# A small product on quarters of the matmul array, with its result sent through DRAM: one change to a gated pair of linear attentions

## The chip, the cores and the metric

The kernel runs on one core of a Trainium2 chip. The metric is the device time of one execution in microseconds (us). All runs told of here were in the fast state, at a granted TensorE clock of 1.0 unless the text says otherwise (the granted clock is the share of its full clock that the chip lets TensorE run at). A ratio is the mean time of one kernel's fast runs over the mean of the fast runs of the kernel before in the same rounds, with a 95% interval; it is therefore not quite the ratio of the medians that are quoted beside it.

## The reference, cut to what matters

Two branches, A and B, of linear attention read the same x (2048 rows of 640) with weights of their own. A gate mixes their outputs.

```python
def _A_ref(x, wqkv, wo):                 # _B_ref is the same with B's weights
    B, S, D = x.shape                    # 1, 2048, 640
    H = 32; Dh = D // H                  # 32 heads of 20
    q, k, v = ...                        # x @ wqkv, split in heads
    phi = lambda t: jnp.where(t > 0, t + 1, jnp.exp(t)) + 1e-6
    pq, pk = phi(q), phi(k)
    kv = jnp.einsum("bhsd,bhse->bhde", pk, v)
    z = jnp.einsum("bhsd->bhd", pk)
    num = jnp.einsum("bhqd,bhde->bhqe", pq, kv)
    den = jnp.einsum("bhqd,bhd->bhq", pq, z)[..., None] + 1e-6
    return ... (num / den) ... @ wo

g = _sigmoid((x * gate_w).sum(-1, keepdims=True))
return g * a + (1 - g) * b
```

The kernel uses that everything behind pq is linear. It first forms G = pk^T x (640 by 640). KV is the part of G and wv within each head, 32 blocks of 20 by 20. Then W' = KV wo (640 by 640) is made once a branch, so that each row tile of the output is one product of the scaled pq with W'.

## The kernel before

A small list scheduler in the file orders the operations. Its order on TensorE is the order of the program text. The parts that the change and the argument touch:

```python
GR = 120      # rows of a unit: six heads
NU = 6        # five units of 120 rows, and a sixth of which 40 are used
...
    # KV: for each unit, wv's columns against G; VectorE masks what is not in a head's block
    def kv_unit(X):
        ...
        for us in ((0, 1, 2, 3), (4, 5)):
            ...
                for i, u in enumerate(us):
                    lo = GR * u if u < 5 else D - GR
                    for c in range(NC):
                        r = e.matmul(
                            PS[0:GR, ps.slot, GR * i : GR * i + GR],
                            WV[X][:, c, lo : lo + GR],
                            gv[:, c, :, lo // 5 : lo // 5 + 24],
                            start=(c == 0),
                            stop=(c == NC - 1),
                        )
...
    # W': one product a unit on the whole array, copied by ScalarE, then copied to its layout
    def wp_unit(X, u):
        ...
            e.matmul(a[0:GR, 0:512], KVL[X][:, u, :], WO[X][:, u, 0:512], start=True, stop=True)
            return e.matmul(a[0:GR, 512:D], KVL[X][:, u, :], WO[X][:, u, 512:D], start=True, stop=True)
        ...
            lambda e: e.activation(WST[X][:, u, :], psw(ps, D)[0:GR, :], ACT.Copy),
        ...
        dma("SP", ..., WP[X][lo // 5 : hi // 5, :, :], WST[X][r:GR, u, :], ...)
...
    # the output: A's part of the first NOA row tiles is kept in SBUF in fp32; B's part is added later
    NOA = 13
    ...
    for u in range(NU):
        wp_unit("B", u)
        if u % 2 == 0:
            o_part(5 + u // 2)
    for t in range(8, NOA):
        o_part(t)
    ...
    for t in range(NOA):
        o_rest(t)                        # B's part, and VectorE's add
    ...
    for t in range(NOA, NT - 1):
        out_unit(t)                      # A and B in one accumulation, ScalarE's copy
    out_last(NT - 1)
```

## Time and profile before

| | before |
|---|---|
| median of the first 3 runs | 188.89 us (188.58 to 189.0) |
| span of the profiled run | 187.6 us |
| TensorE busy | 184.6 us, 98% |
| VectorE, ScalarE busy | 72%, 51% |

TensorE never waits after the first 5.1 us. The first tile of B in the output stage reads the W' of B that was made last. In the lines of profiles below, PE is TensorE, PEld its weight loads, DVE VectorE, ACT ScalarE, POOL GpSimd and SP SyncE; a q behind a name means the engine's instruction queue, and L904 is line 904 of the kernel. The timeline of TensorE in the kernel before shows no gap there (start, duration in us, engine, line, operation, output and inputs, count):

```profile
158.15 1.52 PE L904 MATMUL ps<-WPA,PKA 128*128 128x512 bf16 x10
159.51 0.71 PE L904 MATMUL ps<-WPB,PKA 128*128 128x512 bf16 x4
```

Ten matmuls of one tile are spaced over 1.36 us (their durations overlap, so the group shows 1.52), and 158.15 + 1.36 is 159.51: the first matmul on WPB follows at once.

### The profile page before, as it was taken

To read this page: it belongs to the slowest core of one execution; us is meant where nothing else is said; L and a number is where in the kernel's file an instruction comes from. 1 tells how busy PE (TensorE), PEld (TensorE's weight loads), DVE (VectorE), ACT (ScalarE), POOL (GpSimd) and SP (SyncE) were. 2 spreads that over 40 slices of the span, in tenths; PEclk is the share of its full clock that TensorE was granted. 3 is DMA by queue.
4 is the path that set the end of the run, shared out by engine and by line. 5 is a ranking of instruction groups with operands and counts; after the bars stand their busy time and mean duration, and the time that the engine had idled before them with its cause. 6 is when DMAs were issued, how large, how long until landed. Compare 5 with 4: busy or idle time off the path is not lost.

```text
span 187.6 us, 3202 instructions
## 1 busy us (share of the span) xinstructions
PE 184.6 (98%) x1261; PEld 107.9 (58%) x1261; DVE 135.4 (72%) x260; ACT 95.6 (51%) x171; POOL 0.8 (0%) x8
## 2 busy tenths in 40 slices
PE   8999999999999999999999999999999999999995
PEld 4555555555555656665557556655556655555552
DVE  2388888888833555487798999879996999965600
ACT  5365655556554546544675667877524594100012
POOL 1000000000000000000000000000000000000000
PEclk9999999999999999999999999999999999999999
DMA  7999999996001011011701222540015165132322
GB/s 185 293 163 158 252 392 364 344 214 136 4 0 35 0 38 35 0 35 24 92 10 31 56 49 48 124 116 3 0 35 118 32 153 134 39 140 105 136 79 70
DMA packets 36301, 19.89 MB, mean 106 GB/s; under 512 B 25630, under 2 KB 36286, under 8 KB 36286
## 3 DMA queue, kind: packets, MB, share of 16 engines
q1 hardware_dynamic: 35844, 19.48, 41.6%
q8 instruction: 10, 0.16, 0.4%
q10 hardware_dynamic: 442, 0.20, 0.4%
q14 instruction: 5, 0.04, 0.1%
HBM read 9.39 MB, written 2.62 MB: 64 GB/s over the span
## 4 chain that ended last, share of the span: by engine, by line
PE 96%; DMA 2%; SPq 0%; DVE 0%; issue 0%; DVEq 0%
PE ps L904 23%; PE ps L744 23%; PE ps L513 18%; PE ps L618 18%; PE ps L619 5%; PE ps L514 5%; DMA WKW<-in_A_wqkv_dram 2%; PE ps L660 2%; PE ps L698 1%; SPq L343 0%; PE ps L699 0%; DVE TSB L948 0%; DVEq L230 0%; PE ps L494 0%
## 5 line engine op out<-in xcount | busy, mean ns | idle before, releaser
L513 PE MATMUL ps<-WKW,XT 128*128 128x512 bf16 x160 | 44.4, 381 | 0.3 <-DMA WKW<-in_A_wqkv_dram 0.3
L761 ACT ACTIVATE EK<-ps 128x512 bf16<-128x512 f32 x40 | 23.9, 598 | 31.5 <-PE ps L744 29.4
L514 PE MATMUL ps<-WKW,XT 128*128 128x128 bf16 (+1 forms) x160 | 35.2, 220 | 0.0
L546 ACT ACTIVATE EK<-ps 128x640 bf16<-128x640 f32 x32 | 22.4, 704 | 10.8 <-DVE EK L549 5.9
L513 PEld LDWEIGHTS ps<-WKW,XT 128*128 128x128 bf16 x160 | 15.7, 98 | 19.8 <-DMA WKW<-in_A_wqkv_dram 0.6
L744 PE MATMUL ps<-XT,WQA 128*128 128x512 bf16 x100 | 24.5, 379 | 0.0
L744 PE MATMUL ps<-XT,WQB 128*128 128x512 bf16 x100 | 23.7, 379 | 0.0
L618 PE MATMUL ps<-XN,PKB 128*128 128x512 bf16 x80 | 23.5, 379 | 0.0
L618 PE MATMUL ps<-XN,PKA 128*128 128x512 bf16 x80 | 23.5, 379 | 0.0
L771 DVE TENSOR_SCALAR EK<-EK 128x512 bf16<-128x512 bf16 x40 | 11.6, 291 | 14.9 <-ACT EK L761 14.8
L619 PE MATMUL ps<-XN,PKA 128*128 128x129 bf16 x80 | 17.6, 220 | 0.0
L619 PE MATMUL ps<-XN,PKB 128*128 128x129 bf16 x80 | 17.6, 220 | 0.0
L904 PE MATMUL ps<-WPA,EX 128*128 128x512 bf16 x120 | 17.3, 299 | 0.0
L904 PE MATMUL ps<-WPB,PKA 128*128 128x512 bf16 x120 | 16.5, 299 | 0.0
L744 PEld LDWEIGHTS ps<-XT,WQB 128*128 128x128 bf16 x100 | 10.9, 117 | 8.5
L514 PEld LDWEIGHTS ps<-WKW,XT 128*128 128x128 bf16 x160 | 15.8, 98 | 0.0
L549 DVE TENSOR_SCALAR EK<-EK 128x640 bf16<-128x640 bf16 x32 | 10.4, 326 | 7.1 <-ACT EK L546 7.1
L744 PEld LDWEIGHTS ps<-XT,WQA 128*128 128x128 bf16 x100 | 10.6, 117 | 8.1
L618 PEld LDWEIGHTS ps<-XN,PKA 128*128 128x128 bf16 x80 | 9.4, 118 | 7.9
L618 PEld LDWEIGHTS ps<-XN,PKB 128*128 128x128 bf16 x80 | 9.4, 117 | 7.8
L950 ACT ACTIVATE TSB<-ps 128x640 bf16<-128x640 f32 (+1 forms) x3 | 2.0, 668 | 23.2 <-PE ps L904 23.2
L557 DVE SCALAR_TENSOR_TENSOR PKA<-ps,EK 128x640 bf16<-128x640 f32 x16 | 13.2, 825 | 0.6
(77 smaller groups left out, 239.9 us busy)
## 6 DMA issues: line engine op xcount, KB each, us to landing
out_dram<-TSB SPq DMA_DIRECT2D x15, 160.0 KB, 1.8
XN<-in_A_x_dram SPq DMA_DIRECT2D x1, 2240.0 KB, 9.0
WKW<-in_A_wqkv_dram SPq DMA_DIRECT2D x5, 160.0 KB, 4.2
WKW<-in_B_wqkv_dram SPq DMA_DIRECT2D x5, 160.0 KB, 4.0
WQA<-in_A_wqkv_dram SPq DMA_DIRECT2D x1, 800.0 KB, 10.7
WQB<-in_B_wqkv_dram SPq DMA_DIRECT2D x1, 800.0 KB, 11.9
WVA<-in_A_wqkv_dram SPq DMA_DIRECT2D x1, 800.0 KB, 12.7
WVB<-in_B_wqkv_dram SPq DMA_DIRECT2D x1, 800.0 KB, 14.3
```

Of the source, the lines that this page charges most:

```text
L513: e.matmul(a[:, 0:512], l, WK[X][:, c, 0:512], start=(c == 0), stop=(c == NC - 1))
L514: return e.matmul(a[:, 512:w], l, WK[X][:, c, 512:w], start=(c == 0), stop=(c == NC - 1))
L546: op("ACT", lambda e: e.activation(EK[:, ek.slot, :], psw(ps, D), ACT.Exp), act_cost(D), ins=[ps] + first, outs=[ek], name="ke")
L549: lambda e: e.tensor_scalar(EK[:, ek.slot, :], EK[:, ek.slot, :], 1.0, EPS, op0=ALU.min, op1=ALU.add),
L557: lambda e: e.scalar_tensor_tensor(PKt[X][:, t, :], psw(ps, D), 0.0, EK[:, ek.slot, :], op0=ALU.max, op1=ALU.add),
L618: e.matmul(a[:, 0:512], l, XN[:, t, 0:512], start=(t == 0), stop=(t == NT - 1))
L619: return e.matmul(a[:, 512 : D + 1], l, XN[:, t, 512 : D + 1], start=(t == 0), stop=(t == NT - 1))
L660: r = e.matmul(PS[0:GR, ps.slot, GR * i : GR * i + GR], WV[X][:, c, lo : lo + GR], gv[:, c, :, lo // 5 : lo // 5 + 24], start=(c == 0), st ...
L744: r = e.matmul(PS[:, ps.slot, :], WQ[X][:, c, g::5], XT[:, c, 512 * b : 512 * b + 512], start=(c == 0), stop=(c == NC - 1),)
L761: lambda e: e.activation(EQ[:, eq.slot, :], PS[:, ps.slot, :], ACT.Exp),
L771: lambda e: e.tensor_scalar(EQ[:, eq.slot, :], EQ[:, eq.slot, :], 1.0, EPS, op0=ALU.min, op1=ALU.add),
L904: r = e.matmul(a[:, l0 - lo : h0 - lo], PQ[X, b][:, g, 128 * (t % 4) : 128 * (t % 4) + 128], WP[X][:, g, l0:h0], start=(X == first and g = ...
```

## The change

The intent is to use the array better in W'. A unit of W' has at most 120 rows in six blocks of 20 by 20, so most of the 128 by 128 array multiplies zeros. The change takes 60 by 60 blocks and puts four of them on the four 64 by 64 quarters of the array. All of W' of a branch is then done in two bursts of 320 output columns each. W' goes from its staging tile to its layout through DRAM, in five stores and one load, in place of six copies inside SBUF. KV gets full 128-column weights and a narrow last unit. Fifteen row tiles of A are kept instead of 13. Four padding rows that the 64-row layout needs are loaded.

```diff
-                    lo = GR * u if u < 5 else D - GR
                     for c in range(NC):
+                        lo, n, w = (GR * u, 128, 24) if u < 5 else (540, 104, 8)
                         r = e.matmul(
-                            PS[0:GR, ps.slot, GR * i : GR * i + GR],
-                            WV[X][:, c, lo : lo + GR],
-                            gv[:, c, :, lo // 5 : lo // 5 + 24],
+                            PS[0:n, ps.slot, GR * i : GR * i + NC * w],
+                            WV[X][:, c, lo : lo + n],
+                            gv[:, c, :, 24 * u : 24 * u + w],
...
+    def wp_burst(X, half):
+        ps = [Buf("wp", "ps", 2) for _ in range(2)]
+        lo = HALF * half
+        def fn(e):
+            for k in range(3):
+                for a, b in ((0, 192), (192, HALF)) if k == 1 else ((0, HALF),):
+                    for t in range(4 * k, min(4 * k + 4, 11)):
+                        c, r, u = t // 2 % 2, t % 2 if t < 10 else 1, t // 2
+                        w, p = (64 - 4 * r, HR) if t < 10 else (40, 40)
+                        d = HR * r if t < 10 else 0
+                        o = PS[64 * c : 64 * c + p, ps[r].slot : ps[r].slot + 2, :].rearrange("p a b -> p (a b)")
+                        x = e.matmul(
+                            o[:, HALF * k + a : HALF * k + b],
+                            KVL[X][64 * r : 64 * r + w, u, d : d + p],
+                            WO[X][64 * r : 64 * r + w, u, lo + a : lo + b],
...
+            for c in range(2):
+                st(X, r, c, 3 * r, 2 if c else 3, HR, 120 * c + HR * r)
+            if r:
+                st(X, r, 2, 5, 1, 40, 600)
+        if half == 1:
+            last_ld[0] = dma("SP", "wpl" + X, WP[X][:, :, :], WPD[X].rearrange("(p g) n -> p g n", g=NC), 819200, ...)
...
-    NOA = 13
+    NOA = 15
...
-    for u in range(NU):
-        wp_unit("B", u)
-        if u % 2 == 0:
-            o_part(5 + u // 2)
+    wp_burst("B", 0)
+    o_part(5)
+    o_part(6)
+    wp_burst("B", 1)
+    o_part(7)
     for t in range(8, NOA):
         o_part(t)
+    ft_op[2].behind, ft_op[3].behind = last_st[0], last_ld[0]
```

Cut are the masks, the loads of wo by halves of 60 rows, the scheduler's constants and the pads, and some reordering: KV of B one tile earlier, W' of A at other places of its loop, one copy raised in priority, two scalings of B held behind adds. The last line orders two of B's four factor transposes (the DMA transposes of the scaling factors of its row blocks) on SyncE's queue: the third behind the last store, the fourth behind the load.

More of the change, by code (lines that the diff above doesn't have):

```diff
@@ L20 @@
 NU = 6
+HR = 60
+HALF = 320
 def _bf16_bits(a):
@@ L30, in _consts @@
     p = np.arange(128)[:, None]
-    bd = (p // 20 == np.arange(24)[None, :] // 4).astype(np.float32)
-    return _bf16_bits(bd)
-CW = 24
+    q, m = p % 64, np.arange(24)[None, :]
+    bd = np.where(p < 64, (q >= 4) & ((q - 4) // 20 == m // 4), (q < 60) & (3 + q // 20 == m // 4))
+    be = q // 20 == m[:, 0:8] // 4
+    return _bf16_bits(np.concatenate([bd, be], axis=1).astype(np.float32))
+CW = 32
 XS_W = 672
@@ L40, with __init__ @@
 class Buf:
-    def __init__(self, name, pool=None, n=1):
-        self.name, self.pool, self.n = name, pool, n
+    def __init__(self, name, pool=None, n=1, at=(0, 2, 4, 6)):
+        self.name, self.pool, self.n, self.at = name, pool, n, at
         self.writers, self.readers = [], []
@@ L107, in can @@
                 w = max(w, d.end + (HOP if d.eng != o.eng or d.dma else 0.0))
+            skip = set()
             for b in o.outs:
                 if b.pool and b.slot is None:
-                    got = self.pick(b, w)
+                    got = self.pick(b, w, skip)
                     if got is None:
@@ L113, in can @@
                     w = max(w, got[0])
+                    skip |= set(range(got[1], got[1] + b.n))
             return w
@@ L144, in run @@
                 at[e] = w + o.dma[0]
-                o.end = max(w + o.dma[0] + 1500.0, bus[0]) + o.dma[1] / o.dma[2]
+                o.end = max(w + o.dma[0] + o.dma[3], bus[0]) + o.dma[1] / o.dma[2]
                 bus[0] = o.end
@@ L163, in run, with pick @@
         return max(o.end for o in self.ops)
-    def pick(self, b, t):
+    def pick(self, b, t, skip=()):
         pool = self.free[b.pool]
@@ L169, in pick @@
         for x in pool:
-            have[x[1]] = x[0]
+            if x[1] not in skip:
+                have[x[1]] = x[0]
         if b.n == 1:
-            if not pool:
+            if not have:
                 return None
@@ L176, in pick @@
             return best[0], best[3]
-        c = [(max(have[s], have[s + 1]), s) for s in have if s % 2 == 0 and s + 1 in have]
+        c = [(max(have[i] for i in range(s, s + b.n)), s) for s in b.at if all(i in have for i in range(s, s + b.n))]
         return min(c) if c else None
@@ L275, in body @@
     WQ = {X: sb("WQ" + X, [128, NC, D], bf) for X in XS}
-    WV = {X: sb("WV" + X, [128, NC, D], bf) for X in XS}
-    WO = {X: sb("WO" + X, [GR, NU, D], bf) for X in XS}
+    WV = {X: sb("WV" + X, [128, NC, D + 8], bf) for X in XS}
+    WO = {X: sb("WO" + X, [128, NU, D], bf) for X in XS}
     PK = {X: sb("PK" + X, [128, NT * D], bf) for X in XS}
@@ L296, in body @@
     GS = {X: sb("GS" + X, [128, NC, D], bf) for X in XS}
-    KVL = {X: sb("KVL" + X, [GR, NU, GR], bf) for X in XS}
-    WST = {X: WKW[0:GR, i * NU * D : (i + 1) * NU * D].rearrange("p (u f) -> p u f", u=NU) for i, X in enumerate(XS)}
+    KVL = {X: sb("KVL" + X, [128, NU, GR], bf) for X in XS}
+    WST = {X: WKW[:, i * NU * D : (i + 1) * NU * D].rearrange("p (u f) -> p u f", u=NU) for i, X in enumerate(XS)}
     WP = {X: sb("WP" + X, [128, NC, D], bf) for X in XS}
@@ L303, in body @@
     FXT = {"A": WV["A"][:, :, :].rearrange("p c f -> p (c f)")[:, 0:2048].rearrange("p (b s) -> p b s", b=NB), "B": XNf[:, 0:2048].rearrange("p (b s) -> p b s", b=NB)}
-    NOA = 13
+    NOA = 15
     OA = [XNf[:, 2048 + 1280 * i : 3328 + 1280 * i].bitcast(f32) for i in range(6)]
-    OA += [PK["B"][:, 1280 * i : 1280 * i + 1280].bitcast(f32) for i in range(7)]
+    OA += [PK["B"][:, 1280 * i : 1280 * i + 1280].bitcast(f32) for i in range(8)]
+    OA += [XT[:, :, :].rearrange("p c s -> p (c s)")[:, 0:1280].bitcast(f32)]
     NEK, NEQ, NOS = 4, 4, 4
@@ L328, in body @@
     IDN = sb("IDN", [128, 128], bf)
-    BDM = CST[0:GR, 0:24]
+    BDM = CST[:, 0:24]
+    BDE = CST[64:104, 24:32]
     sch = Sched({"ps": 8, "ek": NEK, "eq": NEQ, "os": NOS})
@@ L339, in dma @@
     def dma(q, name, dst, src, nbytes, ins=(), outs=(), after=(), issue=450.0, transpose=False, prio=None):
+        timing = (330.0, 1500.0) if not transpose else (140.0, 1500.0) if loading else (1000.0, 1150.0)
         def fn(e):
@@ L343, in fn @@
                 return e.dma_start(d, src() if callable(src) else src, transpose=transpose)
-        o = op(q, fn, 0.0, ins, outs, after, prio=prio, name=name, dma=(issue, nbytes, 95.0 if transpose else 330.0))
+        o = op(q, fn, 0.0, ins, outs, after, prio=prio, name=name, dma=(issue, nbytes) + timing)
         if loading:
@@ L369, in body @@
     bwv = {X: Buf("wv" + X) for X in XS}
-    bwo = {X: Buf("wo" + X) for X in XS}
+    bwo = {}
     op("DVE", lambda e: e.memset(ONE[:, :], 1.0), 120.0, outs=[bone], name="one")
@@ L386, in body @@
     zgw = op("POOL", lambda e: e.memset(GWZ[:, :], 0.0), 200.0, name="zgw")
+    bpad = {X: Buf("pad") for X in XS}
+    for X in XS:
+        op("POOL", lambda e, X=X: e.memset(WV[X][:, :, 0:4], 0.0), 300.0, outs=[bpad[X]], prio=10**6, name="wvpad")
     bxo = Buf("xo")
@@ L403, in xt_dma @@
             outs=bxt[t0:t1],
-            issue=(t1 - t0) * 850.0,
+            issue=(t1 - t0) * 1250.0,
             transpose=True,
@@ L427, in body @@
     for X in XS:
-        dma("SP", "wv" + X, WV[X][:, :, :], w3(X, 2), 819200, outs=[bwv[X]])
+        dma("SP", "wv" + X, WV[X][:, :, 4 : D + 4], w3(X, 2), 819200, outs=[bwv[X]])
     for X in XS:
-        bo5 = Buf("wo5" + X)
-        dma("SP", "wo" + X, WO[X][:, 0:5, :], wo[X][0:600, :].rearrange("(u p) n -> p u n", p=GR), 768000, outs=[bwo[X]])
-        dma("SP", "wo5" + X, WO[X][:, 5, :], wo[X][520:640, :], 153600, outs=[bo5])
-        bwo[X, 5] = bo5
+        for r in range(2):
+            bwo[X, r] = Buf("wo")
+            dma(
+                "SP",
+                "wo%s%d" % (X, r),
+                WO[X][4 + HR * r : 64 + HR * r, 0:5, :],
+                wo[X][0:600, :].rearrange("(u r p) n -> r p u n", r=2, p=HR)[r],
+                384000,
+                outs=[bwo[X, r]],
+            )
+        bwo[X, 2] = Buf("wo")
+        dma("SP", "wopad" + X, WO[X][0:4, 0:5, :], wo[X][0:4, :].unsqueeze(1).to_broadcast([4, 5, D]), 25600, outs=[bpad[X]])
+        dma("SP", "wo2" + X, WO[X][64:104, 5, :], wo[X][600:640, :], 51200, outs=[bwo[X, 2]])
     loading.clear()
@@ L633, in g_unit @@
             outs=[z],
+            prio=-1,
             name="zc",
@@ L643, in g_unit @@
             outs=[bgs[X, g]],
-            issue=850.0,
+            issue=1250.0,
             transpose=True,
@@ L652, in kv_unit, with out @@
         gv = GS[X][:, :, :].rearrange("p c (g m) -> p c g m", g=NC)
-        for us in ((0, 1, 2, 3), (4, 5)):
-            ps = Buf("kv", "ps")
-            def fn(e, us=us, ps=ps):
-                for i, u in enumerate(us):
-                    lo = GR * u if u < 5 else D - GR
-                    for c in range(NC):
-                        r = e.matmul(
-                            PS[0:GR, ps.slot, GR * i : GR * i + GR],
-                            WV[X][:, c, lo : lo + GR],
-                            gv[:, c, :, lo // 5 : lo // 5 + 24],
-                            start=(c == 0),
-                            stop=(c == NC - 1),
-                        )
-                return r
-            o = op("PE", fn, 5 * len(us) * mm_cost(GR), ins=[bwv[X]] + [bgs[X, g] for g in range(NC)], outs=[ps], name="kv" + X)
-            if X == "A":
-                kv_op[X].append(o)
+        def out(src, u0, n, w, mask, r0, r1):
             b = Buf("kvl")
             bkvl[X].append(b)
-            n = len(us)
             op(
                 "DVE",
-                lambda e, us=us, ps=ps, n=n: e.tensor_tensor(
-                    out=KVL[X][:, us[0] : us[0] + n, :].rearrange("p u (m g) -> p u g m", g=NC),
-                    in0=PS[0:GR, ps.slot, 0 : GR * n].rearrange("p (u g m) -> p u g m", u=n, g=NC),
-                    in1=BDM.unsqueeze(1).unsqueeze(1).to_broadcast([GR, n, NC, 24]),
+                lambda e: e.tensor_tensor(
+                    out=KVL[X][r0:r1, u0 : u0 + n, 0 : w * NC].rearrange("p u (m g) -> p u g m", g=NC),
+                    in0=src().rearrange("p (u g m) -> p u g m", u=n, g=NC),
+                    in1=mask.unsqueeze(1).unsqueeze(1).to_broadcast([r1 - r0, n, NC, w]),
                     op=ALU.mult,
                 ),
-                dve1(GR * n),
+                dve1(w * NC * n),
                 ins=[ps, bcst],
@@ L688, in kv_unit @@
             )
-    bwp = {}
-    bwpm = {X: [] for X in XS}
-    def wp_unit(X, u):
-        ps = Buf("wp", "ps", 2)
-        def fn(e):
-            a = psw(ps, D)
-            e.matmul(a[0:GR, 0:512], KVL[X][:, u, :], WO[X][:, u, 0:512], start=True, stop=True)
-            return e.matmul(a[0:GR, 512:D], KVL[X][:, u, :], WO[X][:, u, 512:D], start=True, stop=True)
-        op(
-            "PE",
-            fn,
-            mm_cost(512) + mm_cost(128),
-            ins=[bkvl[X][u // 4], bwo[X] if u < 5 else bwo[X, 5]],
-            outs=[ps],
-            name="wp%s%d" % (X, u),
-        )
-        b = Buf("wst")
-        op(
-            "ACT",
-            lambda e: e.activation(WST[X][:, u, :], psw(ps, D)[0:GR, :], ACT.Copy),
-            act_cost(D),
-            ins=[ps],
-            outs=[b],
-            prio=-1,
-            name="wpc",
-        )
-        bwp[X, u] = b
-        d = Buf("wpm")
-        bwpm[X].append(d)
-        r = 80 if u == 5 else 0
-        lo, hi = GR * u, min(D, GR * u + GR)
-        dma(
-            "SP",
-            "wpm%s%d" % (X, u),
-            WP[X][lo // 5 : hi // 5, :, :],
-            WST[X][r:GR, u, :],
-            1280 * (hi - lo),
-            ins=[b],
-            outs=[d],
-            issue=850.0,
@@ new lines, in kv_unit, with fn @@
+        for us in ((0, 1, 2, 3), (4, 5)):
+            ps = Buf("kv", "ps")
+            def fn(e, us=us, ps=ps):
+                for i, u in enumerate(us):
+                    for c in range(NC):
+                        lo, n, w = (GR * u, 128, 24) if u < 5 else (540, 104, 8)
+                        r = e.matmul(
+                            PS[0:n, ps.slot, GR * i : GR * i + NC * w],
+                            WV[X][:, c, lo : lo + n],
+                            gv[:, c, :, 24 * u : 24 * u + w],
+                            start=(c == 0),
+                            stop=(c == NC - 1),
+                        )
+                return r
+            o = op("PE", fn, 5 * len(us) * 55.0, ins=[bwv[X], bpad[X]] + [bgs[X, g] for g in range(NC)], outs=[ps], name="kv" + X)
+            if X == "A":
+                kv_op[X].append(o)
+            n = min(us[-1], 4) - us[0] + 1
+            out(lambda ps=ps, n=n: PS[:, ps.slot, 0 : GR * n], us[0], n, 24, BDM, 0, 128)
+            if 5 in us:
+                out(lambda ps=ps: PS[64:104, ps.slot, GR : GR + 40], 5, 1, 8, BDE, 64, 104)
@@ new lines, in body @@
+    bwst = {(X, r): Buf("wst") for X in XS for r in range(2)}
+    bwps = {X: [] for X in XS}
+    WPD = {X: nc.dram_tensor("wps" + X, [D, D], bf, kind="Internal").ap() for X in XS}
+    bwpm = {X: [Buf("wpm")] for X in XS}
+    def wp_burst(X, half):
+        ps = [Buf("wp", "ps", 2) for _ in range(2)]
+        lo = HALF * half
+        def fn(e):
+            for k in range(3):
[9 more added lines that the diff above has]
+                            WO[X][64 * r : 64 * r + w, u, lo + a : lo + b],
+                            start=True,
+                            stop=True,
+                        )
+            return x
+        op("PE", fn, 640.0, ins=bkvl[X] + [bwo[X, i] for i in range(3)] + [bpad[X]], outs=ps, name="wp%s%d" % (X, half))
+        for r in range(2):
+            dst = WST[X][0:124, 3 * r : 3 * r + 3, lo : lo + HALF]
+            src = lambda r=r: psw(ps[r], 3 * HALF)[0:124, :].rearrange("p (k n) -> p k n", k=3)
+            op(
+                "ACT",
+                lambda e, dst=dst, src=src: e.activation(dst, src(), ACT.Copy),
+                act_cost(3 * HALF),
+                ins=[ps[r]],
+                outs=[bwst[X, r]],
+                prio=-1 if X == "A" else None,
+                name="wpc",
+            )
+            if half == 0:
+                continue
+            for c in range(2):
[3 more added lines that the diff above has]
+        if half == 1:
+            last_ld[0] = dma("SP", "wpl" + X, WP[X][:, :, :], WPD[X].rearrange("(p g) n -> p g n", g=NC), 819200, ins=bwps[X], outs=bwpm[X], prio=-1)
@@ new lines, in body, with st @@
+    last_st, last_ld = [None], [None]
+    def st(X, r, c, slot, n, rows, row):
+        h = 64 * min(c, 1)
+        b = Buf("wps")
+        bwps[X].append(b)
+        last_st[0] = dma(
+            "SP",
+            "wps%s%d%d" % (X, r, c),
+            bass.AP(tensor=WPD[X].tensor, offset=WPD[X].offset + D * row, ap=[[D, rows], [240 * D, n], [1, D]]),
+            WST[X][h : h + rows, slot : slot + n, :],
+            1280 * rows * n,
+            ins=[bwst[X, r]],
+            outs=[b],
+            issue=450.0,
@@ L833, in den @@
                 after=[red_op[b]] if b in red_op else (),
-                issue=900.0,
+                issue=1250.0,
                 transpose=True,
@@ L874, in den @@
                 after=kv_op[X],
-                issue=900.0,
+                issue=1250.0,
                 transpose=True,
@@ L920, in o_mm @@
         )
-    boa = {}
+    boa, adds = {}, {}
     def o_part(t):
@@ L938, in o_post @@
         if eng == "ADD":
-            op(
+            adds[t] = op(
                 "DVE",
@@ L1004, in f @@
             elif g == 2:
+                if k == 1:
+                    wp_burst("A", 0)
                 q_next(1)
-                wp_unit("A", 2 * k)
-                wp_unit("A", 2 * k + 1)
             elif g == 3:
+                if k == 0:
+                    wp_burst("A", 1)
                 q_next(2)
@@ L1022, in body @@
     den("B")
+    kv_unit("B")
     o_part(3)
-    kv_unit("B")
     o_part(4)
-    for u in range(NU):
-        wp_unit("B", u)
-        if u % 2 == 0:
-            o_part(5 + u // 2)
+    wp_burst("B", 0)
[3 more added lines that the diff above has]
+    o_part(7)
     for t in range(8, NOA):
         o_part(t)
+    ft_op[2].behind, ft_op[3].behind = last_st[0], last_ld[0]
     for b in range(3):
@@ L1041, in body @@
     out_last(NT - 1)
+    for h in range(2):
+        pqs_op["B", 3, h].behind = adds[3 + h]
     span = sch.run()
```

## The prediction

> **What bounds the kernel now.** I read the page's busy shares first, then the slices, then the chain that ended last, then the waits of TensorE, then the groups and the timeline around the two places that the change touches. The busy shares, the first two rows of slices and the chain:
>
> ```profile
> PE 184.6 (98%) x1261; PEld 107.9 (58%) x1261; DVE 135.4 (72%) x260; ACT 95.6 (51%) x171; POOL 0.8 (0%) x8
> ...
> PE   8999999999999999999999999999999999999995
> ...
> PE 96%; DMA 2%; SPq 0%; DVE 0%; issue 0%; DVEq 0%
> PE ps L904 23%; PE ps L744 23%; PE ps L513 18%; PE ps L618 18%; PE ps L619 5%; PE ps L514 5%; DMA WKW<-in_A_wqkv_dram 2%; PE ps L660 2%; PE ps L698 1%; SPq L343 0%; PE ps L699 0%; DVE TSB L948 0%; DVEq L230 0%; PE ps L494 0%
> ```
>
> TensorE is on the chain for 96% of 187.6 us. The page cautions that a busy PE is not PE at its peak, so the waits of TensorE come next. They are all there are:
>
> ```profile
> PE ps L444 <- DVE ONE L372: 0.4, 1, 0.4
> PE ps L513 <- DMA WKW<-in_A_wqkv_dram: 0.3, 1, 0.3
> ```
>
> Both lie in the first 5.1 us. From there to the last matmul the kernel is one stream of matmuls, and a change pays only by shortening the stream or costs by opening a hole in it. The groups that the change touches are W' (lines 698 and 699) and KV (line 660); the timeline shows what they cost as spacing, which is what counts, since durations overlap:
>
> ```profile
> L698 PE MATMUL ps<-WOB,KVLB 120*120 120x512 bf16 x6 | 2.1, 380 | 0.0
> L699 PE MATMUL ps<-WOB,KVLB 120*120 120x128 bf16 x6 | 1.3, 217 | 0.0
> L660 PE MATMUL ps<-GSB,WVB 128*120 128x120 bf16 x30 | 1.8, 218 | 0.0
> ...
> 115.22 0.38 PE L698 MATMUL ps<-WOA,KVLA 120*120 120x512 bf16 x1
> 115.44 0.22 PE L699 MATMUL ps<-WOA,KVLA 120*120 120x128 bf16 x1
> 115.49 0.38 PE L698 MATMUL ps<-WOA,KVLA 120*120 120x512 bf16 x1
> 115.70 0.22 PE L699 MATMUL ps<-WOA,KVLA 120*120 120x128 bf16 x1
> 115.76 0.38 PE L618 MATMUL ps<-XN,PKB 128*128 128x512 bf16 x1
> ```
>
> Two pairs of W' take 115.22 to 115.76: 0.27 us a pair of 640 columns, so 2.36 columns per ns at the full granted clock. Twelve pairs: 3.26 us for both branches, 1.7% of the span. That is the whole purse: if W' cost nothing, the gain would stay below 2%. The 30 KV matmuls of branch B run from 143.99 to 145.64: 1.65 us, 55 ns each.
>
> **What the Trainium skill says.** "TensorEngine Tiling (Array Packing)", section Key Properties: 64x64 gives four tiles that load weights and multiply in parallel, and changing the mode drains TensorE. "TensorE: Matmul & The Clock Gate", section Measured speedup vs the span model: a pack lasts about one matmul plus 4 ns for each further tile; its 16-tile pack was 10.6 times faster. The same page, section Weight-path perf modes, ties fast weight load to full 128-column weights; the trace before agrees in direction: loads of 128 columns in the output stage take 98 ns, loads of 120 columns 132 to 135. No tile smaller than the array runs before, so neither the parallelism nor the drain shows in this trace. "DMA: Bandwidth & Descriptors", section Anatomy of one DMA: about 2 us of each DMA are fixed, mostly the write's receipt (a fit for another issuing path). The 160 KB stores to the output here land after a median 1.8 us, which agrees; this matters because W' now goes out to DRAM and back, two such latencies in a row where there was one.
>
> **The change, part by part.** (1) *W' on quarters.* Removed: 3.26 us. Added: four bursts. In each, 11 blocks (60 rows by 60 columns, one of 40) times 320 columns go four abreast in three rounds; the middle round is cut in two at a bank's end. If four really run abreast a burst streams 320 + 192 + 128 + 320 = 960 columns, 0.41 us at 2.36 columns per ns. To this come two changes of mode and weight loads that can't be pulled ahead across them. Estimate: about 0.12 us each, as a matmul of 120 columns lasts 218 ns where its spacing is 55, and a drain exposes most of this difference. That is 0.65 us a burst; the diff's own planning constant is 640 ns. Four bursts: 2.6 us. Gain: 3.26 - 2.6 = 0.65 us.
>
> (2) *KV.* 25 matmuls keep 120 columns; the five of the last unit go from 120 to 40. At 55 ns before and perhaps 30 to 45 after (the 104-column weight load, not the 40 columns, then limits), the gain is 5 x 10 to 25 ns, twice: about 0.15 us.
>
> (3) *Evictions.* ScalarE copied 12 x 0.70 us; now 8 copies of 960 columns. From 598 ns at 512 and 704 at 640 columns the slope is 0.83 ns per column, so 0.97 us each: 7.8 instead of 8.4 us, off the path. VectorE's mask goes from two operations per branch (1.50 and 0.91 us) to three (1.50, some 0.61 and 0.41 on the same slope): nearly the same sum.
>
> (4) *Fifteen kept tiles.* The matmuls of the output (line 904) stay 320 in number and shape. Two row tiles change from copies on ScalarE (0.70 us) to a kept copy and an add on VectorE (0.82 us); in the output stage VectorE still has 0.53 us idle per tile of 1.36 us, so this is hidden. What it buys is time: between the last W' of B and the first tile that reads it, there were five o tiles (6.8 us); now eight (10.9 us).
>
> (5) *wo.* The loads are issued at 28 to 37 us and first read after 115; the two extra clears of the WV pads on GpSimd are nothing against its 0.8 us. Cost 0.
>
> The sum on TensorE: -0.65 - 0.15 = -0.8 us, if no hole opens.
>
> **Holes and rivals.** *W' of B comes late.* From the end of the last burst, say t = 0: 0.2 for the matmul's tail, the two copies done by about 2.2 (one earlier eviction may stand before them), five stores of 0.4 to 0.8 us issue each, the last at about 3.7, landing about 5.7; the load of 800 KB, issued on its receipt, then takes perhaps 4 to 4.7 us (2240 KB landed in 9.0 us here), so about 10 to 10.5. Needed at 10.9. The slack is under 1 us, and SyncE issues in order with the transposes of the factors in between. *For a hole*: two serial latencies, transposes that took 2.6 us to land. *Against*: the tile count was plainly raised to cover it. A hole would be 0.3 to 1.5 us and would eat the gain: 188.4 to 189.6. I give it three in ten. A's round trip has some 14 us and is safe.
>
> *The quarters do not run abreast* (weight loads serialise, or two streams out of the same partitions share a port): 3520 columns in sequence are 1.49 us a burst, 6.0 in all, so 2.7 us worse than before: 191.5. For it: no trace here shows quarters. Against: the skill's measured packs. One in twenty; half-way, a burst at 0.9, would make the change a wash, at 189.0.
>
> *PSUM.* A burst wants four of the eight banks at once. At the second burst of A, near 124.3 us, line 618's next accumulator holds two, the previous one is read by ScalarE (123.05, 0.73 us) and then by the VectorE copy that the trace shows at 124.36, and a q tile holds one until about 124.7. The raised priority of that copy speaks for its author having seen this. A hole of 0.1 to 0.3 us, once.
>
> **Range and chances.** 188.89 - 0.8, plus some 0.2 expected from the holes, is 188.3. A clean run with cheap drains is 187.5; the late load or half-abreast quarters give 189.5. Faster by over 2% needs 185.1, more than W' and KV's savings can give: 0.02. Slower by over 2% needs 192.7, both bad rivals together: 0.03. Within 2%: 0.95.
>
> **What would show it.** Right: each burst's first matmul to the next ordinary matmul is 0.6 to 0.7 us; the waits of TensorE after 6 us stay empty or name one short wait; ordinary matmuls keep their spacing; line 904 keeps 320 matmuls. Wrong in size: bursts near 0.45 (then 187.5) or 0.9. Wrong in kind: a wait of line 904 on the DMA into WPB before the first tile of B, bursts of 1.5 us, or a wait of a burst on ScalarE or on VectorE's small copy. If the span moves with none of these, some other stage was reordered and my reading of the stream was incomplete.

## The result, and the profile after

The changed kernel ran at a median of 188.41 us (six runs, 188.13 to 188.73), the kernel before at 188.88 us (six runs, 188.39 to 189.59). The ratio is 0.9975, interval 0.9953 to 0.9997: the same within 2%, and a little faster. A second set of rounds, told below, gave 0.9960 (0.9948 to 0.9972).

The page of the changed kernel, busy shares and the chain that ended last:

```profile
PE 184.0 (98%) x1297; PEld 106.6 (57%) x1297; DVE 137.4 (74%) x264; ACT 95.2 (51%) x167; POOL 0.8 (0%) x10
...
PE 92%; DMA 4%; ACT 2%; issue 0%; DVE 0%; SPq 0%; DVEq 0%
```

The chain has left TensorE for 8% of the span, where before it was 4%. The waits of TensorE (who waited for whom, us in total, times, longest) say where:

```profile
PE ps L467 <- DVE ONE L383: 0.4, 1, 0.4
PE ps L955 <- DMA WPB<-wpsB: 0.3, 1, 0.3
```

The second line is new. It is the first tile of B waiting for the load of its W'. Here is a burst of W' in the timeline of TensorE, with the matmuls on both sides of it:

```profile
115.87 0.22 PE L642 MATMUL ps<-XN,PKB 128*128 128x129 bf16 x1
116.02 0.60 PE L738 MATMUL ps<-WOA,KVLA 64*60 64x320 bf16 x15
116.55 1.27 PE L795 MATMUL ps<-XT,WQB 128*128 128x512 bf16 x5
117.66 0.38 PE L641 MATMUL ps<-XN,PKB 128*128 128x512 bf16 x1
```

The matmul at 115.87 has 129 columns and would be followed after 0.055 us, at 115.92 (call that the slot of the next one); the burst starts at 116.02. The five matmuls of 512 columns behind the burst need 1.08 us elsewhere in the trace, so with the next matmul at 117.66 they should have started at 116.58. From 115.92 to 116.58 is 0.66 us: that is what a burst takes out of the stream. The other three bursts also start 0.09 to 0.10 us after their slot.

The same view at the place where the kernel before had no gap, and the chain of waits behind it (start, us, what):

```profile
156.97 4.24 PE L955 MATMUL ps<-WPA,PKA 128*128 128x512 bf16 x30
161.49 0.70 PE L955 MATMUL ps<-WPB,PKA 128*128 128x512 bf16 x4 [0.28 <-DMA WPB<-wpsB]
...
152.88 3.61 DMA wpsB<-WKW
...
156.62 4.73 DMA WPB<-wpsB
...
161.49 1.52 PE ps L955 x10
```

Three kept tiles from 156.97 end their slots at 156.97 + 3 x 1.36 = 161.05. The first matmul on WPB starts at 161.49. The hole is 0.44 us; the bracket says 0.28, because the trace's ends of matmuls lie past their slots. The chain names the two legs of the trip: the store that lands last takes 3.61 us, then the load takes 4.73 us.

**A measure without the start.** The first matmul on XN and PKA begins at 48.50 us in the trace before and at 48.24 in the trace after, and in the fourteen traces anywhere from 48.04 to 48.62. The kernel before and b_noa15, which share their start, differ by 0.40 us there, so scatter alone makes differences of this size. So I compare a stretch: from that matmul to the start of the last group of five matmuls in the trace. Before: 185.04 - 48.50 = 136.54 us. After: 184.30 - 48.24 = 136.06 us. Without its hole of 0.44 the changed kernel has 135.62 us, so the stream of matmuls is 0.92 us shorter and the hole takes 0.44 of it back. What is left, 0.48 us, is what the medians show (0.47).

Of the 0.92 us KV brings 0.24. Its 30 matmuls take from 141.94 to 143.47 us in the changed trace, 1.53 us against 1.65, twice:

```profile
141.94 1.69 PE L703 MATMUL ps<-GSB,WVB 128*128 128x120 bf16 x30
143.47 0.70 PE L955 MATMUL ps<-WPA,EX 128*128 128x512 bf16 x4
```

The rest, 0.68 us, is W': 3.26 - 0.68 = 2.58, or 0.645 us for each of the four bursts, which agrees with the 0.66 us read off above to 0.02 us.

### The profile page after: what moved, and what is told of

It is laid out like the page before. It is cut to its first block, busy times and chain, and to the rows that moved or that the text cites. A ratio compares the mean times of both kernels' runs of the same rounds, so it can differ in the third digit from the quotient of the medians.

```text
span 186.8 us, 3273 instructions
## 1 busy us (share of the span) xinstructions
PE 184.0 (98%) x1297; PEld 106.6 (57%) x1297; DVE 137.4 (74%) x264; ACT 95.2 (51%) x167; POOL 0.8 (0%) x10
## 4 chain that ended last, share of the span: by engine, by line
PE 92%; DMA 4%; ACT 2%; issue 0%; DVE 0%; SPq 0%; DVEq 0%
PE ps L795 23%; PE ps L536 19%; PE ps L641 18%; PE ps L955 18%; PE ps L642 5%; PE ps L537 5%; DMA WPB<-wpsB 3%; DMA wpsB<-WKW 2%; PE ps L703 2%; PE ps L467 1%; ACT WKW L753 1%; PE ps L738 1%; ACT PKB L979 1%; PE ps L480 1%; DVE TSB L999 0%
## 5 line engine op out<-in xcount | busy, mean ns | idle before, releaser
L580 DVE SCALAR_TENSOR_TENSOR PKB<-ps,EK 128x640 bf16<-128x640 f32 x16 | 13.2, 825 | 0.6
```

The costliest lines, as they stand in the source:

```text
L580: lambda e: e.scalar_tensor_tensor(PKt[X][:, t, :], psw(ps, D), 0.0, EK[:, ek.slot, :], op0=ALU.max, op1=ALU.add),
```

## The experiments

Eleven variants and a repeat of the changed kernel, all with correct results. "Stretch" is the measure above, "hole" the time by which the first matmul on WPB comes after its slot, both from the one trace of each kernel. Runs between two rules shared a chip and the runs of the kernel before (188.81, 188.82 and 188.94 us).

| kernel | median us | ratio to before (95%) | stretch | hole | stretch less hole |
|---|---|---|---|---|---|
| before | | | 136.54 | 0.00 | 136.54 |
| changed | 188.41 | 0.9975 (0.9953 to 0.9997) | 136.06 | 0.44 | 135.62 |
| --- | | | | | |
| fill | 188.02 | 0.9967 (0.9948 to 0.9985) | 135.62 | 0.00 | 135.62 |
| fx2 | 188.46 | 0.9988 (0.9963 to 1.0014) | 135.62 | 0.00 | 135.62 |
| early | 189.30 | 1.0036 (1.0001 to 1.0072) | 137.88 | 2.27 | 135.61 |
| direct | 189.60 | 1.0042 (1.0027 to 1.0056) | 137.12 | 1.50 | 135.62 |
| --- | | | | | |
| noa13 | 192.74 | 1.0179 (1.0142 to 1.0215) | 140.29 | 3.00 | 137.29 |
| b_noa15 | 188.75 | 0.9997 (0.9980 to 1.0014) | 136.53 | 0.00 | 136.53 |
| kv120 | 188.09 | 0.9962 (0.9944 to 0.9980) | 135.83 | 0.12 | 135.71 |
| pads | 188.27 | 0.9970 (0.9953 to 0.9988) | 135.92 | 0.30 | 135.62 |
| --- | | | | | |
| after_again | 188.07 | 0.9960 (0.9948 to 0.9972) | 135.71 | 0.09 | 135.62 |
| fillfx2 | 188.19 | 0.9963 (0.9946 to 0.9981) | 135.62 | 0.00 | 135.62 |
| double | 189.79 | 1.0045 (1.0031 to 1.0060) | 137.49 | 0.21 | 137.28 |
| serial | 188.36 | 0.9970 (0.9958 to 0.9983) | 135.97 | 0.25 | 135.72 |

The last column is the check on the whole reading: eight traces of kernels that keep the changed stream of matmuls give 135.61 or 135.62 once their own hole is taken off.

**Filler before B's first tile (fill).** Five matmuls of the last row tile, which need only A, are issued before the first tile of B instead of at the end.

```diff
+    early = Buf("o", "ps")
+    o_mm("A", NT - 1, early, 0, 512)
...
-            ps = Buf("o", "ps")
-            for X in XS:
+            ps = Buf("o", "ps") if lo else early
+            for X in XS if lo else ("B",):
```

> The changed kernel, but A's five 512-column matmuls of the last row tile (1.08 us) are issued ahead of B's first tile into a bank that stays open to the end. Theory: the only loss is the hole before B's first tile (0.44 us between the end of the fifteenth kept tile at 161.05 us and the first matmul on WPB at 161.49 us), so the hole closes and the time falls by 0.3 to 0.5 us against the changed kernel, to about 188.0 us; no wait of TensorE on WPB is left. Rival (the hole is bookkeeping of modelled matmul ends, or the final copy of 512 columns now ends later and gives the gain back): within 0.1 us of the changed kernel.

The wait is gone from the trace, and the stretch is 135.62: what the hole cost in the first trace came back in full, so it was real time and not bookkeeping. The timed runs don't resolve it. The median is 188.02 us with runs from 187.74 to 188.8, and its ratio of 0.9967 lies between the two ratios of the changed kernel itself.

**The third factor transpose behind the load (fx2).**

```diff
-    ft_op[2].behind, ft_op[3].behind = last_st[0], last_ld[0]
+    ft_op[2].behind, ft_op[3].behind = last_ld[0], last_ld[0]
```

> The changed kernel, but the third factor transpose of B is issued behind the load of WPB, not between its stores and its load. Theory that this transpose slows the round trip of B (store 3.6 us and load 4.7 us, against about 2.9 and 4.3 us for A with no transpose beside it): WPB lands 0.4 to 1.0 us sooner, the hole of 0.44 us shrinks to 0.1 or less, the time falls by 0.3 to 0.4 us. Rival (bytes and fixed latency alone set the round trip): store and load keep their times within 0.2 us, and so does the hole.

The hole is gone from this trace too: tiles of A run up to the slot at 161.00 us, and there the first matmul on WPB starts.

```profile
157.74 3.42 PE L955 MATMUL ps<-WPA,PKA 128*128 128x512 bf16 x24
161.00 1.19 PE L955 MATMUL ps<-WPB,PKA 128*128 128x512 bf16 x6
```

Measured from the first matmul on XN and PKA, the load is issued 108.1 us in, against 108.4 in both traces of the unaltered changed kernel, so the transpose beside the stores costs some 0.3 us. The load itself took 4.4 us, against 4.7 and 4.3, which tells nothing. So the theory holds for about 0.3 us of the stores and is not shown for the load. The timed runs scatter from 187.95 to 189.66 and show no gain.

**Each half stored at once (early).** The stores of a half of W' follow its own burst, ten half-size stores a branch.

```diff
-            if half == 0:
-                continue
...
-            WST[X][h : h + rows, slot : slot + n, :],
+            WST[X][h : h + rows, slot : slot + n, lo : lo + HALF],
```

> The changed kernel, but each half of W' is stored as soon as its burst is copied, so that only half the bytes remain to be stored after the second burst; ten stores a branch instead of five. Theory that the bytes of the last stores count: the last store lands 0.5 to 1 us sooner and the hole is gone (-0.3 to -0.4 us). Rival (a fixed latency per store and issue on SyncE): the landing of the last store moves by under 0.3 us, the hole stays at 0.2 us or more.

The first half of the theory came true. Counted from the first matmul on XN and PKA, the last landing of a store that the trace holds comes at 107.4 us, 0.85 us sooner than in the changed kernel. But the hole did not go, it grew. The chain of waits shows the third transpose's issue in front of the load, and a load that took long:

```profile
155.80 0.51 SPq L354
...
156.69 6.87 DMA WPB<-wpsB
```

The stores did shorten, to a median of 1.8 and 2.0 us from issue to landing instead of 3.1 and 3.2. But eight of the ten were issued only from 151.0 to 155.1 us, the third transpose stood behind them in SyncE's queue until 156.3 us, and the load behind that. It left at 108.1 us of the same count, only 0.3 us sooner than in the changed kernel: most of what was won in landing was lost in issue. The hole grew by the load alone. Why it took 6.9 us, where branch A's took 4.4 in the same trace, was not isolated. A transpose was issued 1.6 us ahead of it and another right behind it. The six timed runs lie at 188.45, 188.59, 189.16, 189.44, 190.60 and 190.64 us, further apart than those of any other kernel here, which fits a landing that varies between executions of one program. The profiled run is the slowest of them. The two fastest have spans of 186.8 and 187.1 us, like the changed kernel's 186.6 to 187.1, so they can hardly have had a hole of 2.27 us.

**No trip through DRAM (direct).** Eleven copies a branch from the staging tile into W'.

```diff
-            bass.AP(tensor=WPD[X].tensor, offset=WPD[X].offset + D * row, ap=[[D, rows], [240 * D, n], [1, D]]),
-            WST[X][h : h + rows, slot : slot + n, :],
+                WP[X][lo : lo + rows // NC, :, :],
+                WST[X][h : h + rows, slot + j, :],
...
-            last_ld[0] = dma("SP", "wpl" + X, WP[X][:, :, :], ...)
```

> The changed kernel without the trip through DRAM: eleven copies a branch from the staging tile straight into W' in SBUF. Theory that two latencies in a row are what is late: one latency falls away, and the hole closes, -0.3 to -0.4 us. Rival (issue on SyncE: the kernel before showed 0.77 us for each such copy, 11 x 0.77 = 8.5 us from 151.3 us, landing near 162.5 us): the hole grows from 0.44 to 1 to 1.5 us, and the time to 189.0 to 189.5 us. I hold the rival to be more likely.

The rival was right. In the view by tile of WPB (count, shortest, median and longest time of an issue in ns, first and last start in us), followed by the waits of TensorE:

```profile
L354 SPq DMA_DIRECT2D WPB<-WKW x11: 682/765/791, 151.5 to 159.6; - x11
...
PE ps L955 <- DMA WPB<-WKW: 1.3, 1, 1.3
```

Eleven issues of 0.765 us take SyncE until 160.3 us; the hole is 1.50 us. The trip through DRAM costs two latencies, but it spares the queue, and against eleven copies it is the shorter way.

**Thirteen kept tiles (noa13).**

```diff
-    NOA = 15
+    NOA = 13
```

> The changed kernel with 13 kept row tiles of A, as before the change. Theory that the two tiles more are what covers the trip of W' through DRAM: 2 x 1.36 us of matmuls move from before the hole to after it, so the hole grows from 0.44 to about 3.1 us and the time by 2.7 us, to about 191.1 us. Rival (the kept tiles only trade copies of ScalarE for adds of VectorE, and W' would land in time anyway): within 0.3 us of the changed kernel.

The direction and the hole of 3.00 us came as expected, but the time is 192.74 us, 4.3 us over the changed kernel instead of 2.7. Three of the four runs, at 192.68 to 193.0 us, had a mean granted clock of 0.991; the fourth had 1.000 and took 191.16 us, which is the time expected. The table by stretches (length, then busy time and count of PE, PEld, DVE, ACT and POOL; the column PEclk stands before the DMA share and GB/s) shows what happened in one of the three:

```profile
core 0: us, PE busy (x) PEld busy (x) DVE busy (x) ACT busy (x) POOL busy (x), PEclk, DMA share, GB/s
158.00:161.50 3.50, 0.68 (x6) 0.24 (x5) 0.91 (x2) 0.77 (x2) 0.00 (x0) 1.00 0.88 253
161.50:163.00 1.50, 1.48 (x9) 0.83 (x10) 0.00 (x0) 0.00 (x0) 0.00 (x0) 0.81 0.05 11
163.00:165.00 2.00, 2.00 (x9) 0.96 (x8) 0.82 (x1) 0.00 (x0) 0.00 (x0) 0.50 0.00 0
165.00:167.00 2.00, 1.95 (x14) 0.98 (x13) 0.82 (x1) 0.00 (x0) 0.00 (x0) 0.79 0.23 82
167.00:169.00 2.00, 2.00 (x17) 1.17 (x16) 1.00 (x2) 0.00 (x0) 0.00 (x0) 1.00 0.23 82
```

The matmuls resumed at 161.52 us at full clock. From 162.42 to 165.83 us the granted clock was 0.50, then 1.0 again: 3.41 us at half speed lose 1.71 us. The stretch without the hole is 137.29 us, 1.67 longer than in the others, so the slow clock accounts for the rest of the loss, on top of the hole. In the trace of "early" a hole of 2.27 us left the clock at 1.00.

**Fifteen kept tiles in the kernel before (b_noa15).**

```diff
-    NOA = 13
+    NOA = 15
...
-    OA += [PK["B"][:, 1280 * i : 1280 * i + 1280].bitcast(f32) for i in range(7)]
+    OA += [PK["B"][:, 1280 * i : 1280 * i + 1280].bitcast(f32) for i in range(8)]
+    OA += [XT[:, :, :].rearrange("p c s -> p (c s)")[:, 0:1280].bitcast(f32)]
```

> The kernel before with 15 kept tiles, this part of the change alone. There the last copy into WPB was issued at 155.5 us and the first tile of B at 159.5 us waited for nothing, so theory: no change, within 0.15 us of the kernel before, no new wait of TensorE. Rival (two adds more on VectorE, 0.82 us each, delay the scaling of B's last block, or the extra tiles open something earlier): over 0.3 us either way.

A ratio of 0.9997 and a stretch of 136.53 against 136.54: this part alone does nothing. With noa13 this shows what the two tiles buy: cover for the trip of W'.

**The last KV unit at 120 columns (kv120).**

```diff
-                        lo, n, w = (GR * u, 128, 24) if u < 5 else (540, 104, 8)
+                        lo, n, w = (GR * u, 128, 24) if u < 5 else (540, 104, 24)
...
-                            gv[:, c, :, 24 * u : 24 * u + w],
+                            gv[:, c, :, min(24 * u, 104) : min(24 * u, 104) + w],
```

> The changed kernel with the last KV unit again at 120 columns instead of 40 (80 of them thrown away). Theory: 30 matmuls then need 1.65 us again instead of the 1.53 us of the changed kernel, which is +0.12 us of TensorE a branch and +0.24 us in the span if the hole keeps its size; the hole can't absorb it, because B's copies start later too. Rival (the weight load of 104 columns was the limit of the short matmuls, or the hole absorbs it): the KV stretch within 0.05 us of 1.53 us, or the span unchanged.

The stretch without the hole is 135.71, so it is only 0.09 us that came back, 0.045 a branch, not 0.12. The other 0.075 a branch stays gained although all 30 matmuls stream 120 columns as before: their spacing went from 55 ns to 1.53 + 0.045 = 1.575 us over 30, 52.5 ns, and the single records show 52 to 53 ns for each. What did change for them is their weights, 128 columns instead of 120 (104 in the last unit). The weight loads of the 25 last 97 to 98 ns, where those of 120 columns lasted 133 to 135.

The last unit says more. In the changed kernel its matmuls of 40 columns start 48 to 49 ns apart (but for one gap of 29), though 40 columns at 2.36 a ns are only 17 ns. With the same weights of 104 columns and 120 columns to stream, here in kv120, they start 52 to 53 ns apart. So there the weights set the pace in the first case and the streamed columns in the second. 48 ns over 104 weight columns is 0.46 ns each, and 120 of them make 55 ns, the spacing of the kernel before. This reading, that the change took the weights out of the way, accounts for all three spacings; no run varied the weights of the 25 alone.

**The pads cleared on GpSimd (pads).**

```diff
-        dma("SP", "wopad" + X, WO[X][0:4, 0:5, :], wo[X][0:4, :].unsqueeze(1).to_broadcast([4, 5, D]), ...)
+        op("POOL", lambda e, X=X: e.memset(WO[X][0:4, 0:5, :], 0.0), 3000.0, outs=[bpad[X]], prio=10**6, ...)
```

> The changed kernel with the four padding rows of wo cleared on GpSimd instead of loaded. Theory: GpSimd has nothing else after the first 1.2 us and the rows are first read after 115 us, so the time stays within 0.15 us of the changed kernel; only GpSimd's busy time grows by a few us. Rival: something at the start waits for GpSimd (the identity or the ScalarE constant), and the first matmul on weights starts later by over 0.3 us.

GpSimd spends 2.75 us on each of the two clears in the first 6.5 us, no wait of TensorE names it, and the time is 188.27 us. Loading the padding rows instead of clearing them is worth nothing here.

**The changed kernel once more (after_again).**

> The changed kernel once more, word for word, in the same rounds as the combination below. Both theories: 188.2 to 188.6 us. Its trace tells how constant the hole before B's first tile is: if the landing of WPB jitters (4.3 to 4.7 us in the traces so far), the hole lies anywhere between 0.1 and 0.5 us.

It ran at 188.07 us (188.94 for the kernel before; five runs, 187.96 to 188.35), a little under the expected range. The hole in its trace is 0.09 us, with a load of 4.3 us. So the first trace's 0.44 us was at the large end of a scatter.

**Both mends (fillfx2).** The edits of fill and of fx2 together.

> The changed kernel with both mends: A's 512 columns of the last tile as filler before B's first tile, and the third factor transpose behind the load of WPB. Theory: with the filler alone no wait is left in the trace, so the second mend adds nothing to the median: 187.9 to 188.1 us, 0.3 to 0.5 us under the changed kernel; it can only narrow the spread. Rival (some executions of the filler kernel still waited): a median 0.1 to 0.3 us lower than the filler alone showed.

No hole, a stretch of 135.62, and a median of 188.19 us where the unaltered kernel had 188.07 in the same rounds. The theory was right that the second mend adds nothing. Nor does the pair beat the changed kernel by anything that these runs resolve: the hole it removes was only 0.09 us in that call, and the runs of these two kernels spread over 0.4 and 1.2 us. No version is shown to be faster than the changed kernel.

**Every matmul of a burst twice (double).**

```diff
-            for k in range(3):
+            for k in (0, 1, 2, 0, 1, 2):
```

> The changed kernel with every matmul of the bursts issued twice (same results). It divides a burst's 0.65 us into streaming and fixed cost. Theory (four abreast, the mode changes cost a fixed part): a second pass costs its 960 columns, 0.41 us, and up to 0.5 us with its weight loads; bursts of 1.05 to 1.15 us, the span +1.7 to +2.0 us less what the hole absorbs. Rival (no fixed part, weight loads are the limit): the second pass costs the full 0.65 us, +2.6 us.

The burst in the timeline, to be set against 116.02 to 116.55 above:

```profile
116.01 1.02 PE L738 MATMUL ps<-WOA,KVLA 64*60 64x320 bf16 x30
116.96 1.27 PE L795 MATMUL ps<-XT,WQB 128*128 128x512 bf16 x5
```

It lasts 0.95 us instead of 0.53. The second pass costs 0.42 us, and over all four bursts the stretch without holes grows by 1.66 us, 0.415 us each: the 960 columns at 2.36 a ns give 0.41. So the four quarters stream abreast, weight loads cost next to nothing beside them, and of a burst's 0.66 us some 0.24 is fixed. The time rose by 1.72 us against after_again in the same rounds.

**The same matmuls quarter by quarter (serial).**

```diff
-            for k in range(3):
+            for cc, rr, k in [(c, r, k) for c in range(2) for r in range(2) for k in range(3)]:
...
+                        if (t // 2 % 2, t % 2 if t < 10 else 1) != (cc, rr):
+                            continue
```

> The changed kernel with the same 15 matmuls of a burst in the order of the quarters: all of one quarter, then all of the next. Theory (matmuls start in program order, and only neighbours on different quarters overlap): 11 x 320 columns stream one after the other, 1.49 us and up a burst instead of 0.53; the span +3.5 to +4.5 us. Rival (the quarters have queues of their own and run abreast whatever the order): bursts of 0.5 to 0.7 us, the span unchanged.

My theory fell; the rival was right. The busy time of the matmuls on WOA and KVLA in stretches of 0.08 us of the serial program (length, busy time, number of matmuls under way in it, granted clock, DMA share, GB/s):

```profile
116.00:116.08 0.08, 0.00 (x0) 1.00 0.00 0
116.08:116.16 0.08, 0.06 (x4) 1.00 0.00 0
116.16:116.24 0.08, 0.08 (x4) 1.00 0.00 0
116.24:116.32 0.08, 0.08 (x8) 1.00 0.00 0
```

Four matmuls are under way in the first stretch that has any. In this program the first four matmuls are all of one quarter and would have to run one after the other. The individual records make it plain: four matmuls of 320 columns start at 116.103, 116.116, 116.130 and 116.140 us, and the one of 192 columns that stands second in the program starts at 116.261. The second and the fourth to start have weights of 60 rows, where the first four of the program all have 64. The first three gaps, 13, 14 and 10 ns, fit matmuls that are handed out in program order to quarters which start them by themselves: the quarters have 4, 4, 3 and 4 matmuls, and in the interleaved order of the changed kernel neighbours start 3 to 4 ns apart. The last matmul of the program still started last, at 116.437. The burst costs 0.025 us more than in the interleaved order (0.10 us in the stretch, over four).

## Why the prediction was right

The prediction was 188.3 us in a range of 187.4 to 189.5; the first measurement gave 188.41 and the second 188.07.

- **The bound.** That only the stream of matmuls and the holes in it count is shown by the last column of the table. Variants that changed queues, tiles or pads moved the time by their hole alone; the slow clock of noa13 is the one addition.
- **Step 1, W' on quarters.** 0.65 us a burst was predicted, 0.645 to 0.66 measured, and "double" confirms both terms: 0.41 of streaming, and 0.24 of fixed cost for entering and leaving, the "about 0.12 us each" of the estimate. That 0.12 was a judgment ("most of" a difference of 0.163 us), so that it fits this closely is in part luck. The gain was 0.68 us for the predicted 0.65.
- **Step 2, KV.** The term was mis-sized. 0.15 us was predicted, 0.24 measured. The narrow unit gave 0.09 us, less than the step allowed it: its matmuls, held up by their weights as the step said, start 48 ns apart and not 30 to 45. The other 0.15 came from the shorter spacing, 52.5 ns, of matmuls that "keep 120 columns", which the step had put at zero, although the prediction itself had set loads of 98 ns beside loads of 132 to 135 ns.
- **Step 3, evictions.** The copies of 960 columns took 0.97 us, as worked out, and stayed off the path. The masks on VectorE took 1.50, 0.57 and 0.27 us for B, the two small ones less than the slope said.
- **Steps 4 and 5, kept tiles and wo.** Right: b_noa15 and pads show both parts to cost nothing alone, and noa13 shows what the tiles buy.
- **The late W' of B.** This rival was given three chances in ten and a hole of 0.3 to 1.5 us. It is the one that came. The four traces with the changed kernel's order on SyncE and around B's first tile (changed, after_again, kv120, pads) have holes of 0.44, 0.09, 0.12 and 0.30 us: it came in all four, and twice it was shorter than the least that was reckoned. The wait of the first tile of B on this DMA is on the prediction's list of signs of being "wrong in kind", while "one short wait" is on its list of signs of being right; both lists fit the first trace. The term that was short is the landing of the stores, 3.6 us for the last where about 2 was reckoned: the prediction had leaned on the 1.8 us of the 160 KB stores to the output, and the stores of W' of 150 and 225 KB had medians of 2.8 to 3.2 us. The load, put at 4 to 4.7 us, took 4.3 to 4.7. That the expected loss of 0.2 us was about right is luck: a likely short hole took the place of an unlikely longer one.
- **Quarters that do not run abreast; a burst that waits for banks.** Neither came. No wait of a burst on ScalarE or VectorE is in the trace, and all four bursts start the same 0.09 to 0.10 us after their slot.

The sum on TensorE was thus -0.92 us for the predicted -0.8, and the holes took 0.1 to 0.4 for the predicted 0.2. The net of the two traces of the changed kernel, -0.48 and -0.83 us, lies on both sides of the predicted -0.6. What stays open is why the load of "early" took 6.9 us.

## What to carry to other kernels

When one engine's stream is the bound, split every trace into the length of that stream and the holes in it, and leave out the start: here this resolved 0.05 us where the timed runs of a kernel scattered by 0.2 to 2.2 us. Small products on quarters should stand in bursts, because entering and leaving costs a fixed 0.24 us, as much as some 570 columns of streaming at 2.36 a ns. A slack of a few tenths of a us behind two DMA latencies in a row is no slack: give the stream other work to do there, and keep the hole well under 3 us, for one of 3.00 us cost another 1.67 us through the clock, and three of that kernel's four runs paid it.

## What the Trainium skill lacked or had wrong

- **Order of matmuls on different tiles.** "TensorE: Matmul & The Clock Gate", section The mechanism (Part 3), says that matmuls are strict FIFO, "pc-monotone in start AND end". In the serial program they were not: the matmul that stands second (192 columns) started at 116.261 us, after three of other quarters that stand behind it in the program (116.116, 116.130 and 116.140). The same order gave 0.56 us from the first small matmul to the next ordinary one instead of the 1.49 us and up that strict order would need.
- **The price of changing the mode.** "TensorEngine Tiling (Array Packing)", section Key Properties, says that a change drains TensorE, without a number. Here entering and leaving 64 by 64 cost 0.24 us together, 0.10 of it ahead of the first small matmul.
- **What full-width weights are worth in a dense stream.** "TensorE: Matmul & The Clock Gate", section Weight-path perf modes, gives it for the load. Here the spacing of matmuls with 120 columns was 55 ns with weights of 120 columns and 52.5 ns with weights of 128; that the weights are the cause is the reading that fits, as kv120 told, and not a test of its own.
- **How short an idle gap slows the clock.** "TensorE: Matmul & The Clock Gate", section Why this matters for your kernels, warns of gaps over about 3 us, and the page's Part 1 gives an idle window of about 3.4 us. Here 3.00 us was enough in the trace of noa13 (granted clock 0.50 for 3.41 us, 1.67 us lost), one of its four runs kept the full clock, and the 2.27 us of "early" were not enough.
